# A fused attention, convolution and Fourier-mixing kernel: first batch reordered, some small operations on another engine

## The chip, the cores and the metric

The kernel runs on one core of one Trainium2 chip. The metric is the device time of one execution in microseconds (us). Before the change the median of three runs is 663.12 us (661.9 to 669.41).

The core has five engines with a queue each, worked off in order: PE (TensorE, matrix products), DVE (VectorE), ACT (ScalarE), POOL (GpSimd) and SP (SyncE, which here only issues transfers). Engines wait for each other through semaphores.

## The reference

Three parts follow each other, for four batches of 768 tokens and 384 channels (8 heads of 48):

```
f = sigmoid(f_logit)                                   # (B, H, S, D)
for t in range(S):                                     # gated linear attention
    state = f[t] * state + outer(k[t], v[t])
    y[t]  = q[t] @ state
x = y with the heads side by side                      # (B, S, 384)

gate = sigmoid(sum over 5 taps of conv_w[k] * x[t - 4 + k])
x = (gate * (x @ w_val)) @ w_out

u  = x + real(fft over tokens and channels of x)
un = (u - mean) / sqrt(var + 1e-6)
out = u + relu(un @ w_ch1) @ w_ch2                     # 384 -> 1536 -> 384
```

## The kernel before

**Attention.** Each batch is cut into six chunks of 128 tokens. The products of the decays f inside a chunk are made by `Prep` (line 405) for two chunks at a time: two ACT operations make the logarithm of f (exponential, then logarithm), a DVE scan sums it along the tokens, two more exponentials give `e` and the new `f`, and four products `scaled` multiply them into `qk` (the tile of q and k). A letter of `E0`, `E1` or `E2` (lines 1080 and 1081) says for each of the four whether DVE (v) or POOL (g) does it: `E0` for the first pair, `E1` for the second and third pair (the rest of the first batch), `E2` for all later batches. Three small operations write `ends`, `pends` and `pm`, the decay over a whole chunk. `Prep.load` fetches `f` and `qk`; there are two buffers of each, so the third pair's `qk` can be loaded only when the first pair's is read for the last time, by the outputs of the second chunk.

For a chunk, `scores` multiplies k with q and masks the result (`af` in the first batch), and `outputs` makes the change of the state, the outputs y and the new state `T`, and copies y to `xT`; a transfer moves a part of it to other partitions, and `parts` splits it into two half-precision parts `xhl`. In the first batch the products take float32 operands; `whole` transposes k on PE (tile `ktf`). In later batches operands are split into two half-precision parts (`qkhl`, `vz`), and k is transposed by a transfer (`kt`). `batch` (line 668) runs the chunks in the order: scores of the next chunk, outputs of this one, `parts` of the one before, then `others` and `ahead` for chunks further on: `others` runs the steps of the next `Prep`, `ahead` the `split` of the chunk two ahead and the load of v.

**Gates.** `gates` computes the convolution and the value product. In the first batch four of the six half gates take their convolution from PE, as products with 30 diagonal 128x128 matrices (`fs` in the profile, for the buffer they lie in). `diagonals` (line 227) makes four small vectors (`cwf`, `cwh`) and then the 30 matrices on ACT. Three half gates are done within the attention of the first batch, three in `tail`, which then makes sums and differences of the halves (`even_odd`, tiles `eo` and `gd`) and `mix`es them (Fourier products) into `u`, `un` and `unT`. ACT must load another table of functions between a sigmoid and an exponential or logarithm.

**Weights.** `small_weights` decodes `w_out` (`raw`), `w_val` (`vraw`, `wv`) and the convolution's weights from 64-bit floats, and folds tables into them (`tab`, `wth`, `wtl`, `wch`, `wp`). `mlp_weights` does the same for the 24 pieces `w` of the two large matrices: a load, three DVE operations, two on ACT and one on POOL for each piece, no more than four loads ahead.

**MLP.** `mlp` is the main part of PE's work. `merge` traces it between the attention, gates and mixing of the later batches; it starts with the first `unT`.

**What sets the order.** The program is traced in Python, and a planner then sets each engine's order ahead of time: whenever an engine is free in the planner's own simulation, it takes the ready instruction of the lowest rank, and the rank is the place in the trace. So an instruction that is ready early fills a gap, wherever it was traced. `at(c, r)` gives a block the fixed rank r instead: `LATER` (880) for the weight pieces, `LATER + 200` for the second batch's `others` and `ahead` that are traced in the first batch. `behind` and `issue_after` put an instruction behind another one of the same engine, `after` behind one of any engine. The first exponential of each `Prep` is `behind` the last ACT instruction traced so far. `aside` (line 1032) traces one step of a side job after each step of the first batch, `first` from the small weights, `second` from the pieces, `third` from the diagonals. `keep_warm` issues products with no use, 128x512 each, that keep PE active: `PRE` ahead of the first batch, `WARM` after each of its first 16 steps (`UNTIL`), `W1N` ahead of the first mix. They write a PSUM buffer `c1`, of which there are two, shared with the transposes. All instructions carry the line of a helper (L80), so the tiles tell them apart.

Of the kernel before, what the change touches and what calls it, by code (L numbers as in the profile page):

```python
# [17 lines left out]
ALU = mybir.AluOpType  # L18
# [10 lines left out]
NC = SEQ // CH  # L29
SUB = CH // 2  # L30
GW = SUB + 2
NT = 3
# [194 lines left out]
def diagonals(c):  # L227

    nc, T = c.nc, c.T
    n = KT * TAPS  # L230
    c.fs = T([128, 4, KT, DM], F16, "fs")
    c.diagonal = c.fs.rearrange("p a b d -> p (a b d)")[:, 0:2 * n * 128].rearrange("p (l k t m) -> p l k t m", l=2, k=KT, t=TAPS)
    hi, w = T([128, n], F16, "cwh"), T([128, 2, n], F32, "cwf")
    nc.gpsimd.tensor_scalar(w[:, 1], c.convw.rearrange("p a b -> p (a b)"), CW_SCALE, 1.0, ALU.mult, ALU.mult)
    nc.gpsimd.tensor_copy(hi, w[:, 1])
    nc.gpsimd.tensor_copy(w[:, 0], hi)
    nc.gpsimd.tensor_tensor(w[:, 1], w[:, 1], w[:, 0], ALU.subtract)
    for i in range(n):
        for l in range(2):
            nc.scalar.activation(c.diagonal[:, l, i // TAPS, i % TAPS], c.ident, AF.Copy, scale=w[:, l, i:i + 1])  # L240
        if i % 2:
            yield
    yield
# [68 lines left out]
def token_tables(c):  # L312

    for i in range(4):
        c.nc.gpsimd.dma_start(c.fs[:, i], c.io["fs"][i])
# [89 lines left out]
class Prep:  # L405
# [13 lines left out]
    def steps(self, es):  # L419
# [19 lines left out]
        if t == 0:  # L439
# [8 lines left out]
        cs = slice(t * TC, (t + 1) * TC)  # L448
        nc.gpsimd.tensor_copy(c.ends[:, b, :, cs, :], e[:, :, :, :, SUB + 1].rearrange("p a c h -> p h c a"))
        lo, hi = max(t * TC - 1, 0), (t + 1) * TC - 1  # L450
        pe = c.T([128, hi - lo, NP], F32, "pends", 2)
        nc.gpsimd.tensor_tensor(pe, c.ends[:, b, 1, lo:hi], c.ends[:, b, 0, lo + 1:hi + 1], ALU.mult)
        n = (hi - lo) * NP
        nc.gpsimd.tensor_tensor(
            c.pm[:, b, lo:hi].rearrange("p c a h -> p (c a) h"),
# [17 lines left out]
class Attention:  # L473


    def __init__(self, c):
        self.c = c
        self.preps, self.hl, self.kt, self.v, self.a = {}, {}, {}, {}, {}

# [172 lines left out]
    def parts(self, g, x):  # L652
# [5 lines left out]
        (nc.vector if g == NC - 1 else nc.gpsimd).tensor_tensor(x.hl[:, 1, :, s], xf, x.hl[:, 0, :, s], ALU.subtract)  # L658

    def ahead(self, g):  # L660

        if g >= NB * NC:
            return
        self.split(g)
        if g + 2 < NB * NC:
            self.load_v(g + 2)

    def batch(self, b, x, extra, others):
# [4 lines left out]
        for i in range(NC):  # L673
# [8 lines left out]
            if g + 2 < NB * NC:  # L682
                with at(c, LATER + 200 if b == 0 and g // 2 + 2 >= NT else None):
                    others(g)
                with at(c, LATER + 200 if b == 0 and g + 2 >= NC else None):
                    self.ahead(g + 2)
                if g % 2 and g // 2 + 3 < NB * NT:
                    self.prep(g // 2 + 3)
# [302 lines left out]
def emit(tc, io):  # L991
    c = setup(tc, io)
    with tc.tile_pool(name="sb", bufs=1) as pool, tc.tile_pool(name="ps", bufs=1, space=bass.MemoryType.PSUM) as psum:
# [5 lines left out]
        nc.vector.memset(c.sep.rearrange("p (a w) -> p a w", w=GW)[:, :, 0:1], 0.0)  # L999
        att = Attention(c)  # L1000
        mlp_tiles(c)
        att.prep(0)
# [12 lines left out]
        att.prep(2)  # L1015
        keep_warm(c, PRE)

# [30 lines left out]
        def abc():  # L1048
            for b in range(NB):
# [4 lines left out]
                for n, v in enumerate(att.batch(b, x, todo, others)):  # L1054
                    if b == 0:
                        aside(first, SIDE[n] if n < len(SIDE) else 1)
                        aside(third, 1, None, False)
                        if n >= WFROM:
# [8 lines left out]

                for v in tail(c, b, todo, gate, outs, hook, lambda: token_tables(c) if b == 0 else None):
                    yield v
# [10 lines left out]
E0 = 'vvvv'  # L1080
E1, E2 = 'vgvg', 'gggv'
LO = 'vgv'
# [13 lines left out]
MULTIPLIED = ((0, 0), (0, 1), (0, 2), (1, 0))  # L1096
WARM = 2
LAG = 4000.0
RATIO = 1.1
PRE = 30  # L1100
UNTIL = 16
# [353 lines left out]
```

## Time and profile before

| | |
|---|---|
| median of three runs | 663.12 us |
| the profiled execution | 660.67 us, of which 658.9 us are the span from its first to its last instruction |
| PE busy | 578.2 us (88%) |
| DVE, ACT, POOL busy | 429.9, 292.0, 218.7 us |
| mean granted PE clock | 0.950 of full speed |
| transfers | 53.40 MB, mean 81 GB/s |

The times of rows below are taken in the profiled execution, from the start of its span. "Idle before" is the time that an engine stood still ahead of a group, with what ended it; "issue" means that the profile shows nothing that it waited for. The granted clock is PE's, as a share of full speed; 0.5 is its lower level. Where nothing ran on PE yet, a clock of 1.00 has no record behind it.

### The profile page before, as it was taken

The numbers are of one execution on the slowest core, as the hardware profiler recorded it, in microseconds if no ns is written. First come the engines' busy times: TensorE is split into PE (matmuls) and PEld (weight loads), VectorE is DVE, ScalarE is ACT, GpSimd is POOL, SyncE is SP. The second block draws the span as 40 slices with busy tenths as digits, with TensorE's granted clock in tenths as the row PEclk, the third lists the DMA queues.
The fourth block names the chain that finished last, engine by engine and source line by source line (L and its number), as shares of the span: only waits on it lengthen the run. The fifth ranks groups of instructions, "written<-read, shape, count | busy, mean of one in ns | idle before, by whom it ended". The sixth has DMA issues, their size and how long they took to land.

```text
span 658.9 us, 11989 instructions
## 1 busy us (share of the span) xinstructions
PE 578.2 (88%) x4808; PEld 421.0 (64%) x4808; DVE 429.9 (65%) x710; ACT 292.0 (44%) x526; POOL 218.7 (33%) x242
## 2 busy tenths in 40 slices
PE   1477778188899889999998989999999999999995
PEld 1245666066667666777577766776577868777774
DVE  6358758796968869544669779345588493463661
ACT  3686559443477365312366663211365442121110
POOL 2175446541464361302339351212352212120000
PEclk9689789599899899999979999999999999999998
DMA  8317543922145542003205531003213100041000
GB/s 316 114 30 254 156 155 109 293 79 76 36 89 141 111 139 82 25 1 70 44 19 155 155 89 62 2 1 72 41 43 53 23 25 1 1 73 25 25 26 29
DMA packets 58098, 53.40 MB, mean 81 GB/s; under 512 B 40080, under 2 KB 49552, under 8 KB 58032
## 3 DMA queue, kind: packets, MB, share of 16 engines
q1 hardware_dynamic: 57488, 50.69, 28.0%
q0 software_dynamic: 544, 1.84, 0.9%
q8 instruction: 39, 0.64, 0.4%
q14 instruction: 27, 0.22, 0.1%
HBM read 37.58 MB, written 4.72 MB: 64 GB/s over the span
## 4 chain that ended last, share of the span: by engine, by line
PE 53%; DVE 19%; DMA 9%; issue 6%; POOL 5%; ACT 5%; SPq 1%; DVEq 0%; POOLq 0%; ACTq 0%
PE c L80 33%; PE p L80 20%; DMA qk<-in_qk 6%; DVE gate L80 5%; DVE w L80 4%; DMA w<-in_w_ch 2%; DVE eo L80 1%; DMA xT<-xT 1%; POOL w L80 1%; ACT fs L80 1%; SPq L80 1%; DVE T L80 1%; ACT f L80 1%; POOL qk L80 1%; DVE qkhl L80 1%
## 5 line engine op out<-in xcount | busy, mean ns | idle before, releaser
L80 PE MATMUL c<-unT,w 128*128 128x256 f16 x1296 | 195.6, 276 | 1.2 <-DVE unT L80 1.2
L80 PE MATMUL c<-w,hh 128*128 128x384 f16 x576 | 151.0, 328 | 2.1 <-ACT hh L80 1.3
L80 PEld LDWEIGHTS <-w 128*128 128x128 f16 x1296 | 127.0, 99 | 25.1 <-issue 1.4
L80 PE MATMUL c<-w,hl 128*128 128x384 f16 x288 | 93.0, 328 | 0.0
L80 DVE SCALAR_TENSOR_TENSOR hl<-c,hh 128x512 f16<-128x512 f32 x72 | 49.3, 685 | 62.3 <-ACT hh L80 62.1
L80 ACT ACTIVATE hh<-c 128x512 f16<-128x512 f32 x72 | 42.5, 591 | 98.5 <-PE c L80 94.7
L80 PEld LDWEIGHTS <-hh 128*128 128x128 f16 x576 | 56.2, 98 | 32.0 <-ACT hh L80 1.6
L80 PEld LDWEIGHTS <-gd 128*128 128x128 f16 x468 | 43.8, 97 | 21.7 <-issue 3.5
L80 PE MATMUL p<-wp,gd 128*128 128x388 f16 x216 | 52.7, 327 | 2.5 <-DVE xc L80 1.3
L80 PE MATMUL p<-qkhl 64*128 64x128 f16 x432 | 45.0, 227 | 6.8 <-DVE qkhl L80 5.5
L80 PE MATMUL p<-xhl,wv 128*128 128x384 f16 x216 | 44.1, 328 | 1.8 <-ACT xhl L80 1.0
L80 PE MATMUL p<-ah,vz 128*128 128x128 f16 x288 | 45.3, 228 | 0.0
L80 DVE SCALAR_TENSOR_TENSOR gate<-xT,convw,gate 128x768 f32<-128x768 f32 (+1 forms) x44 | 42.1, 1007 | 4.8 <-ACT gate L80 3.2
L80 POOL TENSOR_TENSOR xhl<-xT,xhl 128x384 f16<-128x384 f32 x23 | 25.1, 1090 | 60.3 <-ACT xhl L80 60.3
L80 PE MATMUL p<-wch,gd 128*128 128x194 f16 x252 | 41.1, 247 | 2.8 <-ACT gd L80 1.4
L80 PEld LDWEIGHTS <-wv 128*128 128x128 f16 x216 | 21.2, 98 | 32.1 <-issue 19.0
L80 PEld LDWEIGHTS <-hl 128*128 128x128 f16 x288 | 28.0, 98 | 19.9 <-issue 2.5
L80 PEld LDWEIGHTS <-qkhl 64*128 64x128 f16 x432 | 22.4, 96 | 27.9 <-issue 15.2
L80 ACT ACTIVATE f<-f 128x1056 f32<-128x1056 f32 x36 | 38.8, 1077 | 2.9 <-DMA f<-in_f 2.6
L80 POOL TENSOR_TENSOR rs<-rs,mhalf 128x2 f32<-128x2 f32 x12 | 8.4, 698 | 93.7 <-DVE rs L80 93.7
L80 PEld LDWEIGHTS <-vz 128*128 128x128 f16 x432 | 37.3, 102 | 3.3 <-issue 0.2
L80 DVE TENSOR_TENSOR a<-p,mask 128x512 f32<-128x512 f32 x36 | 23.2, 682 | 23.3 <-PE p L80 14.4
(161 smaller groups left out, 1086.9 us busy)
## 6 DMA issues: line engine op xcount, KB each, us to landing
qk<-in_qk SPq DMA_DIRECT2D x24, 512.0 KB, 5.8
w<-in_w_ch SPq DMA_DIRECT2D x21, 384.0 KB, 4.4
f<-in_f SPq DMA_DIRECT2D x12, 528.0 KB, 4.6
v<-in_v SPq DMA_DIRECT2D x24, 192.0 KB, 2.6
out_dram<-ot SPq DMA_DIRECT2D x24, 192.0 KB, 2.0
raw<-in_w_out SPq DMA_DIRECT2D x3, 384.0 KB, 4.7
vraw<-in_w_val SPq DMA_DIRECT2D x3, 384.0 KB, 7.9
xT<-xT SPq DMA_DIRECT2D x72, 16.0 KB, 1.8
```

What stands on the lines that cost most here:

```text
L80: r = f(*args, **kw)
```

## The change

The warming products are traced at the very start, ahead of the loads, and there are 20 instead of 30 (`PRE`); after each step of the first batch there is one instead of two (`WARM`). The diagonals' steps start at the sixth step of the first batch (n > 4) instead of the first. The four small operations of `diagonals` go from POOL to DVE, and so do `ends`, `pends` and `pm` of the first `Prep`, and with `E1` the four POOL products of the second and third `Prep` (two each). The first batch's `others` and `ahead` no longer have a rank of their own, but lie where they are traced, with one exception: those of the fifth and sixth chunk (NC - 2 and NC - 1, that is, the second batch's second `Prep`, and the `split` of its first two chunks) are put into a list and traced by `catch_up` only after the last gate of the first batch, with the rank 1080 that they had.

```diff
--- before.py
+++ after.py
@@ -231,10 +231,10 @@
     c.fs = T([128, 4, KT, DM], F16, "fs")
     c.diagonal = c.fs.rearrange("p a b d -> p (a b d)")[:, 0:2 * n * 128].rearrange("p (l k t m) -> p l k t m", l=2, k=KT, t=TAPS)
     hi, w = T([128, n], F16, "cwh"), T([128, 2, n], F32, "cwf")
-    nc.gpsimd.tensor_scalar(w[:, 1], c.convw.rearrange("p a b -> p (a b)"), CW_SCALE, 1.0, ALU.mult, ALU.mult)
-    nc.gpsimd.tensor_copy(hi, w[:, 1])
-    nc.gpsimd.tensor_copy(w[:, 0], hi)
-    nc.gpsimd.tensor_tensor(w[:, 1], w[:, 1], w[:, 0], ALU.subtract)
+    nc.vector.tensor_scalar(w[:, 1], c.convw.rearrange("p a b -> p (a b)"), CW_SCALE, 1.0, ALU.mult, ALU.mult)
+    nc.vector.tensor_copy(hi, w[:, 1])
+    nc.vector.tensor_copy(w[:, 0], hi)
+    nc.vector.tensor_tensor(w[:, 1], w[:, 1], w[:, 0], ALU.subtract)
     for i in range(n):
         for l in range(2):
             nc.scalar.activation(c.diagonal[:, l, i // TAPS, i % TAPS], c.ident, AF.Copy, scale=w[:, l, i:i + 1])
@@ -446,12 +446,13 @@
         scaled(0, 0, 1, e)
         scaled(1, 1, 0, e)
         cs = slice(t * TC, (t + 1) * TC)
-        nc.gpsimd.tensor_copy(c.ends[:, b, :, cs, :], e[:, :, :, :, SUB + 1].rearrange("p a c h -> p h c a"))
+        small = nc.gpsimd if self.u else nc.vector
+        small.tensor_copy(c.ends[:, b, :, cs, :], e[:, :, :, :, SUB + 1].rearrange("p a c h -> p h c a"))
         lo, hi = max(t * TC - 1, 0), (t + 1) * TC - 1
         pe = c.T([128, hi - lo, NP], F32, "pends", 2)
-        nc.gpsimd.tensor_tensor(pe, c.ends[:, b, 1, lo:hi], c.ends[:, b, 0, lo + 1:hi + 1], ALU.mult)
+        small.tensor_tensor(pe, c.ends[:, b, 1, lo:hi], c.ends[:, b, 0, lo + 1:hi + 1], ALU.mult)
         n = (hi - lo) * NP
-        nc.gpsimd.tensor_tensor(
+        small.tensor_tensor(
             c.pm[:, b, lo:hi].rearrange("p c a h -> p (c a) h"),
             pe.rearrange("p c a -> p (c a)").unsqueeze(2).to_broadcast([128, n, 2]),
             c.bmask.unsqueeze(1).to_broadcast([128, n, 2]), ALU.mult)
@@ -475,7 +476,7 @@
 
     def __init__(self, c):
         self.c = c
-        self.preps, self.hl, self.kt, self.v, self.a = {}, {}, {}, {}, {}
+        self.preps, self.hl, self.kt, self.v, self.a, self.later = {}, {}, {}, {}, {}, []
 
     def prep(self, u):
 
@@ -657,6 +658,11 @@
         nc.scalar.activation(x.hl[:, 0, :, s], xf, AF.Copy)
         (nc.vector if g == NC - 1 else nc.gpsimd).tensor_tensor(x.hl[:, 1, :, s], xf, x.hl[:, 0, :, s], ALU.subtract)
 
+    def catch_up(self):
+        for f, g in self.later:
+            f(g)
+        self.later.clear()
+
     def ahead(self, g):
 
         if g >= NB * NC:
@@ -680,10 +686,10 @@
             if i:
                 self.parts(g - 1, x)
             if g + 2 < NB * NC:
-                with at(c, LATER + 200 if b == 0 and g // 2 + 2 >= NT else None):
-                    others(g)
-                with at(c, LATER + 200 if b == 0 and g + 2 >= NC else None):
-                    self.ahead(g + 2)
+                self.later.append((others, g))
+                self.later.append((self.ahead, g + 2))
+                if g not in (NC - 2, NC - 1):
+                    self.catch_up()
                 if g % 2 and g // 2 + 3 < NB * NT:
                     self.prep(g // 2 + 3)
             yield 0
@@ -998,6 +1004,7 @@
         nc.vector.memset(c.sep, 1.0)
         nc.vector.memset(c.sep.rearrange("p (a w) -> p a w", w=GW)[:, :, 0:1], 0.0)
         att = Attention(c)
+        keep_warm(c, PRE)
         mlp_tiles(c)
         att.prep(0)
         load_constants(c)
@@ -1013,7 +1020,6 @@
         att.ahead(1)
         drain(steps[1])
         att.prep(2)
-        keep_warm(c, PRE)
 
         def others(g):
 
@@ -1054,7 +1060,7 @@
                 for n, v in enumerate(att.batch(b, x, todo, others)):
                     if b == 0:
                         aside(first, SIDE[n] if n < len(SIDE) else 1)
-                        aside(third, 1, None, False)
+                        aside(third, int(n > 4), None, False)
                         if n >= WFROM:
                             aside(second, 1, LATER)
                         if n < UNTIL:
@@ -1065,7 +1071,13 @@
                     if b == 0:
                         aside(second, WS, LATER)
 
-                for v in tail(c, b, todo, gate, outs, hook, lambda: token_tables(c) if b == 0 else None):
+                def ready():
+                    if b == 0:
+                        token_tables(c)
+                        with at(c, LATER + 200):
+                            att.catch_up()
+
+                for v in tail(c, b, todo, gate, outs, hook, ready):
                     yield v
 
         c.lag = LAG
@@ -1078,7 +1090,7 @@
 PRELOAD = (0, 3, 4, 5, 8, 11)
 DEC = 'vvvvvvvvvvvv'
 E0 = 'vvvv'
-E1, E2 = 'vgvg', 'gggv'
+E1, E2 = 'vvvv', 'gggv'
 LO = 'vgv'
 HELD = ['vector', 'scalar', 'gpsimd']
 SPO = 'vvv'
@@ -1094,10 +1106,10 @@
 WFROM = 8
 LATER = 880
 MULTIPLIED = ((0, 0), (0, 1), (0, 2), (1, 0))
-WARM = 2
+WARM = 1
 LAG = 4000.0
 RATIO = 1.1
-PRE = 30
+PRE = 20
 UNTIL = 16
 
 
```

## Rows read from the trace of the kernel before

**Rows 1.** Stretches, all engines: length; busy us of PE, PEld, DVE, ACT, POOL; clock; DMA share, GB/s.

```profile
13.30:48.40 35.10, 22.29 (x111) 14.32 (x111) 16.70 (x31) 24.02 (x57) 14.79 (x26) 0.81 0.29 103
...
93.40:97.60 4.20, 0.00 (x1) 0.00 (x0) 4.10 (x6) 2.10 (x3) 4.06 (x3) 0.65 0.22 85
97.60:112.60 15.00, 14.97 (x96) 11.99 (x97) 12.64 (x18) 13.95 (x22) 10.80 (x10) 0.87 0.34 88
112.60:128.70 16.10, 0.30 (x2) 0.07 (x1) 12.21 (x17) 7.51 (x15) 9.55 (x10) 0.58 1.03 314
...
137.10:149.70 12.60, 9.63 (x82) 6.81 (x80) 10.72 (x16) 6.46 (x17) 6.30 (x6) 1.00 0.13 37
149.70:172.70 23.00, 18.66 (x176) 13.55 (x176) 17.49 (x47) 7.38 (x18) 4.67 (x9) 1.00 0.24 70
172.70:340.00 167.30, 159.39 (x1376) 114.06 (x1376) 111.48 (x176) 77.62 (x134) 61.09 (x61) 0.96 0.29 71
```

**Rows 2.** Timeline, POOL, 0 to 50 us: start, duration, operation, [idle before].

```profile
10.47 0.72 POOL L80 COPY ends<-e 128x16 f32<-128x16 f32 x1 [6.46 <-ACT e L80]
21.51 0.19 POOL L80 TENSOR_TENSOR pends<-ends 128x4 f32<-128x4 f32 x1 [10.32 <-issue]
...
41.73 3.55 POOL L80 TENSOR_TENSOR wv<-vraw,wv 128x384 f16<-128x384 f32 x3
...
45.86 1.11 POOL L80 TENSOR_TENSOR qk<-qk,e 128x512 f32<-128x512 f32 x1
```

**Rows 3.** Timeline, ACT, 9 to 50 us.

```profile
10.81 1.07 ACT L80 ACTIVATE f<-f 128x1056 f32<-128x1056 f32 x1
22.88 5.95 ACT L80 ACTIVATE fs<-ident,cwf 128x128 f16<-128x128 f32 x20 [11.00 <-POOL cwf L80]
...
33.40 1.09 ACT L80 ACTIVATE f<-f 128x1056 f32<-128x1056 f32 x1
```

**Rows 4.** Timeline, PE, 0 to 56 us.

```profile
13.35 1.97 PE L80 MATMUL c<-ident,qk 128*128 128x128 f32 x8 [13.35 <-DVE qk L80]
...
29.36 8.54 PE L80 MATMUL c<-sep 128*128 128x512 f16 x30 [9.29 <-ACT ktf L80]
...
48.40 1.71 PE L80 MATMUL p<-qk 64*128 64x128 f32 x16 [0.80 <-POOL qk L80]
```

**Rows 5.** Timeline, DVE, 0 to 50 us.

```profile
42.30 0.89 DVE L80 TENSOR_TENSOR qk<-qk,e 128x512 f32<-128x512 f32 x1 [1.24 <-ACT e L80]
43.41 1.10 DVE L80 TENSOR_TENSOR qk<-qk,f 128x512 f32<-128x512 f32 x1 [0.22 <-ACT f L80]
```

**Rows 6.** The chain that ended last, in order of time: start, us, what.

```profile
9.64 6.89 DMA qk<-in_qk
...
55.60 5.92 DMA qk<-in_qk
```

**Rows 7.** Groups of PE, 38 to 100 us: the warming products.

```profile
L80 PE MATMUL c<-sep 128*128 128x512 f16 x32 | 9.6, 397 | 5.8 <-ACT ktf L80 4.3 <-DVE wtl L80 1.4
```

**Rows 8.** Groups of ACT, 60 to 130 us: busy, mean ns, idle before.

```profile
L80 ACT ACT_TABLE_LOAD x6 | 7.7, 1283 | 0.1
```

**Rows 9.** Timeline, ACT, 60 to 132 us.

```profile
96.01 1.28 ACT L80 ACT_TABLE_LOAD   x1
97.30 1.08 ACT L80 ACTIVATE f<-f 128x1056 f32<-128x1056 f32 x1
```

**Rows 10.** Groups of DVE, 93 to 130 us.

```profile
L80 DVE SCALAR_TENSOR_TENSOR w<-w 128x384 uint32<-128x384 uint32 x16 | 13.4, 860 | 0.3
...
L80 DVE TENSOR_TENSOR_SCAN f<-sep,f 128x1056 f32<-128x1056 f16 x1 | 2.3, 2345 | 0.0
```

**Rows 11.** Groups of POOL, 93 to 130 us.

```profile
L80 POOL TENSOR_TENSOR qk<-qk,e 128x512 f32<-128x512 f32 x4 | 6.1, 1542 | 8.4 <-DMA qk<-in_qk 8.4
```

**Rows 12.** Timeline, SP, 108 to 152 us: issues of transfers.

```profile
118.16 3.11 SPq L80 DMA_TRANSPOSE kt<-qkhl  x1
121.35 1.81 SPq L80 DMA_DIRECT2D xT<-xT  x3
```

## Prediction

> **What bounds the kernel now.** I read the page first: PE is busy for 88% of the span. The stretches come next [rows 1]. From 172.7 us on PE is busy for 159.39 of 167.3 us, so nothing but PE's work counts there, and the change leaves that work alone. What comes before can give time: there PE stands still or works off products with no use, and if the first MLP product starts earlier, the end comes as much earlier.
>
> In 13.3 to 48.4 us no engine is full: PE has 22.29 busy us of 35.1, ACT 24.02, DVE 16.70 [rows 1]. The timelines show why. POOL ends `ends` at 11.19 and starts `pends` at 21.51: 10.32 us in which the profile shows nothing that it waits for [rows 2]. Behind `pends` in its queue lie the four small operations of the diagonals. ACT waits 11.0 us for them, because the planner put 20 diagonals into a gap ahead of everything else; these take 5.95 us, 0.30 each [rows 3]. Behind them stand the copy of the transposed k, for which PE waits 9.29 us, only to run 30 warming products of no use for 8.54, and the exponential of the second pair, at 33.40 [rows 3, 4]. The last link is POOL again: its `qk` product starts only at 45.86, behind its queue of weight splits (`wv` from 41.73), and the next scores, at 48.40, wait for it [rows 2, 4]. DVE's two of the same four products were done at 44.51 [rows 5].
>
> The chain of waits then shows the third pair's `qk` load, at 55.6, issued when the second chunk's outputs release the buffer, which in PE's order stand behind those scores [rows 6]. So what the scores at 48.4 gain goes into the load and into the chunks behind it.
>
> Two more gaps follow: 93.4 to 97.6 (PE without work) and 112.6 to 128.7, 16.1 us with 0.30 of PE [rows 1]. The second batch's decays run around them.
>
> **The change part by part.** Times are against the profiled execution (660.67 us, span 658.9), which is 2.45 us below the median of 663.12.
>
> *A, the start.* With the four small operations on DVE, ACT's wait of 11.0 us goes. The diagonals before the exponential are 28 (20 in the row shown, eight between it and 33.40), 8.3 us at 0.30. Nothing but rank holds them back, so the planner may put them into the same gap; I count 2 of the 8.3. The exponential can't start much before 16.5, where the second `qk` load lands, whose `f` was issued ahead of it [rows 6]; that caps these two at 33.40 - 16.5 = 16.9. Four products on DVE in place of two add 2 x 0.9 to 1.1 us and end near 46.4, so 2 us go from 48.4. Ends: 2 (the products alone) and 18.9; I take 11 + 2 + 2 = 15, near the measured wait.
> The warming products leave PE's way between 29.36 and 37.90, but the scores wait for `qk` anyhow: nothing by themselves. At the start 20 of them, at the mean of 8.54 / 30, take 5.7 us ahead of PE's first product at 13.35 [rows 4], and at twice that still end near it. `ends`, `pends`, `pm` and the four are seven operations of 0.2 us: 1.4 us on DVE, hidden beside waits for loads; 1.4 if the cover goes.
>
> *B, half of the warming in the batch.* 16 products less. The 32 from 38 to 100 us took 9.6 us [rows 7], 0.30 each: 4.8 at most, and nothing where PE waits anyway. Against it the clock can lie lower more often: 97.6 to 112.6 ran at 0.87 after the gap at 0.65 [rows 1], and 6 us more at half speed would cost 3. Ends -4.8 and +3; I take -1.5.
>
> *C, what leaves 93 to 130 us.* ACT loads six tables in 60 to 130 us, 1.283 us each [rows 8]; with the second batch's second `Prep` behind the gates, three in all remain (one ahead of its first `Prep`, one for the gates, one behind them): 3.85 us less. Its four ACT operations (4.4 us, at 1.08 [rows 9]), DVE's scan of 2.35 [rows 10] and three POOL products of 1.54 [rows 11] go too. On SP the transpose of `kt` held 3.11 us ahead of the last `xT` transfer at 121.35, without which the gates can't start [rows 12]. DVE's weight operations took 860 ns in the mean there [rows 10]. How much of this lies on the path to 128.7, no row says. Ends: 3.85 + 4.4 + 2.35 = 10.6 gained, or 2 lost (the second batch's first `Prep`, now with an earlier rank, stands for its load at the head of DVE's queue ahead of chunk work). I take 5: SP's 3.11 and 2 of the table loads.
> After a table load ACT's next operation starts at once: 96.01 + 1.28 is 97.29, and it starts at 97.30 [rows 9]. The Trainium skill (ScalarE: Activation LUTs, "What ACT_TABLE_LOAD costs") adds a drain of some 1.38 us to each load of 1.283, 2.66 together. By it the three would be worth 8.0, and the sum 4.1 lower, an estimate; the trace has no such drain.
>
> *D, where it goes.* ACT order puts the moved `Prep` behind the last gate, on rank 1080, ahead of the sums (`eo`) and the mix. Behind it on ACT wait the `gd` copies, on DVE `eo`, on POOL the `gd` splits. In 137.1 to 172.7, ACT has 13.84 busy of 35.6, POOL 10.97, DVE 28.21 [rows 1]. So the scan and one product, 3.3 us, count on DVE, and I take 3; ends 0 and 14.2 (the slower rival). The loads of the second batch's third `Prep` and of two v tiles also move back on SP; chunks two steps into the second batch read them, and the stretch to 172.7 hides them; without that cover, one load of 5.92 [rows 6].
>
> *E, the third pair's products* all on DVE: two of 0.9 us more in series, two POOL products less beside them: +0.5, ends 0 and 1.8.
>
> *F, handed back.* Ahead of the MLP the weight pieces use DVE, and it has 12.64 of 15.0 and 12.21 of 16.1 us busy [rows 1]. That is 80%: if the pieces alone decided, 0.8 of A's 15 would come back, 12; if they move along with the batch that they are traced with, nothing. I take 3, nearer to nothing, because each piece's DVE work is held behind a batch instruction.
>
> Sum: -15 - 1.5 - 5 + 3 + 0.5 + 3 = -15, 645.7 in the profiled execution, 648 as median.
>
> **The rivals.**
> - *More* (A at 18.9, C at 10.6): -15 - 3.9 - 5.6 = -24.5, 639. For it: idle engines in all gaps. Against: the planner fills gaps, and loads take real time.
> - *The drain* of the page counts as well: 644. Against it stands 97.30.
> - *Handed back* (F at 12): -6, 657. For it: DVE and the piece loads fill 97.6 to 128.7. Against: the pieces are traced with the batch and start earlier with it.
> - *It does not do what it says*: the planner runs DVE's four small operations late and the diagonals stand in the same gap, ACT waiting as before. A is 2, the sum -2, 661.
> - *Slower*: the moved `Prep` and the `split` stand ahead of `gd` in every queue. One table load 1.28, four ACT operations 4.4, the scan 2.35, four POOL products 6.2 in series make 14.2, and two `kt` transposes of 3.11 on SP 6.2: 20.4 instead of D's 3, the sum +2.4, 666. It decides as soon as it exceeds the 18 that the rest nets. For it: rank 1080 is ahead of the mix. Against: `split` reads data that was ready long before.
>
> **How the numbers follow.** Chances: forecast 0.52 (641 to 655), more 0.13, drain 0.02, handed back 0.17 (654 to 661), not done 0.07, slower 0.09. The range 635 to 662 leaves out the lower end of "more" and most of "slower". One per cent is 6.6 us, about what a measurement of this kernel tells from no change. Faster than 656.5: 0.52 + 0.13 + 0.02 + a third of 0.17 = 0.73; slower than 669.7: the upper part of the last case, 0.06; the rest, 0.21, within.
>
> **What would show it.** A: scores of the third chunk near 33 us instead of 48.4, ACT without its 11.0 us wait, no warming products after 13.35. C: three table loads up to the mix, and a gap before the last gates near 11 us. D: `gd` no more than 3 us later behind the last gate. Wrong would be: DVE waiting for what ACT waited for, a gap of 16 us ahead of the last gates as before, or first MLP products at 170 or later.

## The result: 653.2 us, 1.25% faster, and the profile after

The changed kernel takes 653.21 us in the median of 13 runs (647.98 to 658.36), the kernel before 662.01 (13 runs): ratio 0.9875, interval 0.9849 to 0.9901. The forecast was 648 with a range of 635 to 662. The sign was right and the time is inside the range, but the largest term of the sum was far off, and what came behind it made up for a part. The profiled execution is the shortest of the 13 (647.98 us, span 646.1), so its stages show more gain than the median does; a second profile of the same kernel stands under "The kernel after once more". The profiled executions of two versions below, the warming as before and the small operations on GpSimd, are the longest of theirs (660.58 and 666.88 us), and of their stages only the start is read.

From the profile's page of the kernel after: the span and the busy time of the engines.

```profile
span 646.1 us, 11934 instructions
PE 583.7 (90%) x4782; PEld 423.4 (66%) x4782; DVE 434.5 (67%) x721; ACT 287.4 (44%) x523; POOL 212.6 (33%) x231
```

I cut both traces at the same four events: the third chunk's scores, the last gates, the first product of the mix, the first long run of MLP products. Stretches of the kernel before, cut there (columns as in [rows 1]):

```profile
48.40:128.73 80.33, 53.25 (x356) 41.22 (x357) 59.40 (x87) 51.02 (x88) 43.25 (x43) 0.83 0.62 193
128.73:149.73 21.00, 18.00 (x121) 11.25 (x121) 19.12 (x32) 10.28 (x25) 9.77 (x11) 0.92 0.29 85
149.73:172.74 23.01, 18.66 (x177) 13.55 (x177) 17.50 (x47) 7.35 (x18) 4.64 (x9) 1.00 0.24 70
172.74:658.90 486.16, 466.06 (x4045) 340.67 (x4044) 309.80 (x502) 193.21 (x336) 142.04 (x141) 0.98 0.23 56
```

The same stretches of the kernel after, and ahead of them the one up to the scores:

```profile
13.30:43.93 30.63, 15.32 (x75) 12.15 (x75) 23.09 (x41) 26.26 (x60) 14.47 (x20) 0.56 0.32 119
...
43.93:112.87 68.94, 54.22 (x347) 40.67 (x347) 45.61 (x78) 36.04 (x71) 26.88 (x28) 0.87 0.58 189
112.87:138.21 25.34, 20.67 (x122) 12.95 (x121) 23.66 (x39) 16.71 (x33) 15.33 (x13) 0.83 0.45 130
138.21:157.53 19.32, 19.01 (x164) 13.74 (x164) 15.71 (x39) 7.14 (x15) 8.59 (x13) 0.91 0.38 111
157.53:646.10 488.57, 468.38 (x4057) 341.61 (x4056) 319.89 (x513) 195.17 (x343) 143.39 (x144) 0.98 0.23 56
```

The differences are the account of this execution: -4.47 up to the scores, -11.39 from there to the last gates, +4.34 from the gates to the mix, -3.69 and +2.41 in the last two, -12.80 in all (646.1 - 658.9). In the last two PE runs 13 products fewer in the one and 12 more in the other, so they are best read together: -1.28.

The early part, where the forecast saw -15. ACT after (start, duration, operation, [idle before]), to set beside [rows 3]:

```profile
17.40 4.77 ACT L80 ACTIVATE fs<-ident,cwf 128x128 f16<-128x128 f32 x16
...
24.01 1.07 ACT L80 ACTIVATE f<-f 128x1056 f32<-128x1056 f32 x1
24.98 2.14 ACT L80 ACTIVATE fs<-ident,cwf 128x128 f16<-128x128 f32 x7
...
29.26 1.08 ACT L80 ACTIVATE f<-f 128x1056 f32<-128x1056 f32 x1
...
35.76 1.17 ACT L80 ACTIVATE e<-f,small 128x1056 f32<-128x1056 f32 x1
```

The wait of 11.0 us is gone and the second pair's exponential starts at 24.01 instead of 33.40. But the diagonals (`fs`) still run from 17.40 on, 18 of them ahead of that exponential and 12 more between it and `e` at 35.76; tracing them only from the sixth step on did not move them. Then DVE and PE, beside [rows 4, 5]:

```profile
36.95 1.67 DVE L80 TENSOR_TENSOR qk<-qk,e 128x512 f32<-128x512 f32 x2 [4.05 <-ACT e L80]
38.55 3.24 DVE L80 TENSOR_TENSOR_SCAN f<-sep,f 128x1056 f32<-128x1056 f16 x1
41.71 2.16 DVE L80 TENSOR_TENSOR qk<-qk,f 128x512 f32<-128x512 f32 x2
```

```profile
40.17 2.12 PE L80 MATMUL c<-tab,wth 128*128 128x388 f16 x6 [12.16 <-ACT wth L80]
43.93 3.09 PE L80 MATMUL p<-qk 64*128 64x128 f32 x16 [1.64 <-DVE qk L80]
...
112.87 0.48 PE L80 MATMUL p<-xhl,fs 128*128 128x384 f16 x1 [6.65 <-ACT xhl L80]
```

The third pair's scan stands between the second pair's products. PE stands still for 12.16 us, after which the 16 score products take 3.09 us instead of the 1.71 of [rows 4]: the granted clock of 13.3 to 43.93 us is 0.56, against 0.81 for the start in [rows 1]. The third row is the gap ahead of the last gates: 6.65 us, where 112.6 to 128.7 of [rows 1] had almost nothing on PE.

The lower clock reaches on to the third pair's load, which is issued 55.23 us into the kernel before and 53.29 into the kernel after. From the scores to that load PE is busy throughout; before, then after:

```profile
48.40:55.23 6.83, 6.83 (x58) 6.23 (x58) 5.64 (x7) 3.20 (x5) 1.93 (x6) 1.00 0.85 296
```

```profile
43.93:53.29 9.36, 9.36 (x56) 8.40 (x56) 5.60 (x12) 1.14 (x3) 0.42 (x2) 0.68 0.63 226
```

So of the 4.5 us at the scores 1.9 are left at the load.

### The profile page after: what moved, and what is told of

The parts are those of the page before. It is cut to its first block, busy times and chain, and to the rows that moved or that the text cites. A ratio compares the mean times of both kernels' runs of the same rounds, so it can differ in the third digit from the quotient of the medians.

```text
span 646.1 us, 11934 instructions
## 1 busy us (share of the span) xinstructions
PE 583.7 (90%) x4782; PEld 423.4 (66%) x4782; DVE 434.5 (67%) x721; ACT 287.4 (44%) x523; POOL 212.6 (33%) x231
## 4 chain that ended last, share of the span: by engine, by line
PE 53%; DVE 21%; ACT 8%; DMA 8%; issue 4%; POOL 2%; SPq 2%; DVEq 0%; ACTq 0%; POOLq 0%
PE c L80 32%; PE p L80 21%; DVE gate L80 5%; DMA qk<-in_qk 3%; DVE w L80 2%; DVE f L80 2%; DVE qk L80 2%; SPq L80 2%; DVE eo L80 2%; DMA xT<-xT 2%; DMA v<-in_v 2%; ACT fs L80 1%; DVE T L80 1%; DVE vz L80 1%; ACT f L80 1%
## 5 line engine op out<-in xcount | busy, mean ns | idle before, releaser
L80 PEld LDWEIGHTS <-gd 128*128 128x128 f16 x468 | 45.3, 101 | 26.7 <-ACT gd L80 5.0
L80 PE MATMUL p<-wp,gd 128*128 128x388 f16 x216 | 54.0, 335 | 0.9 <-DVE xc L80 0.9
L80 PE MATMUL p<-wch,gd 128*128 128x194 f16 x252 | 43.4, 258 | 6.1 <-ACT gd L80 2.9
L80 PEld LDWEIGHTS <-qkhl 64*128 64x128 f16 x432 | 22.6, 96 | 27.7 <-issue 16.1
L80 POOL TENSOR_TENSOR gd<-eo,gd 128x384 f16<-128x384 f32 x21 | 23.0, 1117 | 50.6 <-ACT gd L80 50.6
L80 POOL TENSOR_TENSOR w<-w 128x384 f16<-128x384 f32 x21 | 26.8, 1284 | 37.9 <-ACT w L80 36.7
```

Source lines behind the costliest of these rows:

```text
L80: r = f(*args, **kw)
```

## The experiments

All times are medians; ratios are to the kernel before, run on the same chip. The first theory: most of what was gained is the deferral, the start gave little. Rival: the start gave it, and the deferral only moves work.

**Without the deferral.** Everything of the change but the deferral (`catch_up` behind the gates goes too, and the second batch's first `Prep` has its old rank again):

```diff
-                self.later.append((others, g))
-                self.later.append((self.ahead, g + 2))
-                if g not in (NC - 2, NC - 1):
-                    self.catch_up()
+                with at(c, LATER + 200 if b == 0 and g // 2 + 2 >= NT else None):
+                    others(g)
+                with at(c, LATER + 200 if b == 0 and g + 2 >= NC else None):
+                    self.ahead(g + 2)
```

> The changed kernel with the second batch's decays and splits of the fifth and sixth step traced where they were before, with their old ranks; all else as changed. Theory 1 (most of the gain is the deferral: between the two traces the last gates come 15.9 us earlier, and only 6.5 of that is there at the last attention product): the gap ahead of the last gates is again 14 to 16 us instead of 6.7, the mix stage gets its 3 us back, the time is 658 to 661 us. Rival (the gain is the start and the warming, and the gap would have shrunk with any earlier start): gap below 10 us, time 652 to 655.

Measured: 654.53 us, 0.9866 [0.9826, 0.9906]: not to be told from the kernel after. The gap ahead of the last gates is 13.54 us (PE, timeline), the stage behind it 20.10.

```profile
121.89 0.48 PE L80 MATMUL p<-xhl,fs 128*128 128x384 f16 x1 [13.54 <-ACT xhl L80]
```

**The deferral alone**, the opposite edit on the kernel before:

> The kernel before with the deferral alone. Theory 1 (deferral is most of the gain): gap ahead of the last gates below 9 us instead of 16.1, mix stage 3 us longer, time 655 to 657. Rival (start and warming are the gain): 660 to 663.

Measured: 658.60 us, 0.9942 [0.9906, 0.9978]. The gap is 6.03 us (PE, timeline):

```profile
121.94 0.48 PE L80 MATMUL p<-xhl,fs 128*128 128x384 f16 x1 [6.03 <-ACT xhl L80]
```

and the stage behind it 24.24 us instead of 21.00. Neither forecast of the time came. The theory fell: the deferral takes 5 to 10 us out of the gap (13.54 against 6.65, and 8.44 in the repeat; 15.83 against 6.03) and gives 3 to 5 of them back behind it; alone it brings 0.6%, and with the fast start of this change nothing that shows.

**The warming as before**: 30 products behind the transposes, two at each step.

```diff
-        keep_warm(c, PRE)
         mlp_tiles(c)
...
         att.prep(2)
+        keep_warm(c, PRE)
...
-WARM = 1
+WARM = 2
-PRE = 20
+PRE = 30
```

> The changed kernel with the warming products as before: 30 behind the first transposes, two after each step. Theory 1: the third chunk's scores wait for the decays, not for PE, so the 30 cost nothing; the second warming product of each step costs what the stretch between the third and the fourth qk load lost, 3 us: 655 to 657. Rival (PE's 12 us without work ahead of the third chunk's scores lower the clock, and the 30 products would keep it up): 651 to 653. Second rival (the 30 products delay the first outputs by 8.5 us as before): 660 or more.

Measured: 651.62 us, 0.9821 [0.9779, 0.9863], no slower than the kernel after, so theory 1 fell. The scores start at 40.32; here the planner has the third pair's scan behind the second pair's products, which made me try that alone (below).

**The small operations back on GpSimd**, the four of the diagonals (one of them shown) and those of the first pair:

```diff
-    nc.vector.tensor_copy(hi, w[:, 1])
+    nc.gpsimd.tensor_copy(hi, w[:, 1])
...
-        small = nc.gpsimd if self.u else nc.vector
+        small = nc.gpsimd
```

> The changed kernel with the diagonals' four small operations and the first decays' three on POOL again. Theory 1: POOL stands still for some 10 us again until the first loads are through, ACT waits for it some 4 to 6 us ahead of the diagonals, the third chunk's scores come 4 to 6 us later than 43.9, and 2 to 5 us of that reach the end: 655 to 658. Rival (the start is not on the path that sets the end): 652 to 654.

Measured: 659.45 us, 0.9967 [0.9931, 1.0003]: most of the gain is gone. POOL's and ACT's timelines of this kernel:

```profile
23.12 0.19 POOL L80 TENSOR_TENSOR pends<-ends 128x4 f32<-128x4 f32 x1 [11.77 <-issue]
```

```profile
24.49 5.65 ACT L80 ACTIVATE fs<-ident,cwf 128x128 f16<-128x128 f32 x19 [12.44 <-POOL cwf L80]
```

POOL's stall and ACT's wait are back as in [rows 2, 3]; the scores come at 53.57 us and the third pair's load at 63.63 instead of 53.29, later than in the kernel before, and more of the time is lost than theory 1 said. So the small operations on DVE are a part that works.

The second theory: the start could have given more, and what it lacks is the diagonals' place (ACT) and the scan's (DVE).

**The diagonals held**, so that each engine really has them behind the batch's last instruction:

```diff
-                        aside(third, int(n > 4), None, False)
+                        aside(third, int(n > 4))
```

> The kernel after with one edit: the 30 diagonals are held, so that ScalarE's order really has them behind the work of the second pair, instead of in its early gap (17.4 to 34.6 us), where they still stand in the kernel after. Theory 1 (they fill a gap in which ScalarE waits for VectorE's chain anyway, so that their place is worth nothing): third chunk's scores at 43 to 45 us as in the kernel after (43.93), third pair's load at 53 to 54, time 652 to 655. Rival 1 (they stand in front of ScalarE's work for the second pair and are what is left of the forecast's 15 us): scores at or ahead of 41, load at or ahead of 50.5, time 648 to 651. Rival 2 (they then stand in front of the exponentials of the first batch's chunks): load as before, but last gates 2 us or more behind the kernel after (112.87), time 655 to 660.

Measured: 643.33 us, 0.9716 [0.9681, 0.9751], 9.1 us under the kernel after measured beside it (652.41); rival 1 came true, and more. This version beats both kernels. ACT, DVE and PE of this kernel:

```profile
26.58 1.18 ACT L80 ACTIVATE e<-f,small 128x1056 f32<-128x1056 f32 x1 [0.20 <-DVE f L80]
...
29.04 0.98 ACT L80 ACTIVATE fs<-ident,cwf 128x128 f16<-128x128 f32 x3
```

```profile
32.17 2.35 DVE L80 TENSOR_TENSOR_SCAN f<-sep,f 128x1056 f32<-128x1056 f16 x1
34.44 1.95 DVE L80 TENSOR_TENSOR qk<-qk,f 128x512 f32<-128x512 f32 x2
```

```profile
36.75 3.09 PE L80 MATMUL p<-qk 64*128 64x128 f32 x16
...
105.19 0.48 PE L80 MATMUL p<-xhl,fs 128*128 128x384 f16 x1 [7.70 <-ACT xhl L80]
```

`e` is 9.2 us earlier than after (35.76), the scores 7.2, the last gates 7.7: the lead stays. The third pair's scan falls into another place too: it ends at 34.52, 0.7 us behind what the product waits for from ACT (33.83), so the 9.1 us are not the diagonals' place alone.

**The diagonals from the first step on, as before**, not held; that part of the change undone alone:

```diff
-                        aside(third, int(n > 4), None, False)
+                        aside(third, 1, None, False)
```

> The kernel after with the diagonals of the convolution traced from the first step of the first batch on, as before, and not held: this one part of the change undone alone. Theory 1 (where they are traced doesn't place them; the planner puts them into ScalarE's early gap either way): the diagonals at the same places within 1 us (16 of them from 17.4 us on, 7 near 25), third chunk's scores at 43 to 44.5 us, third pair's load at 52.5 to 54.5, time within 2 us of the two runs of the kernel after (652.4 and 653.2 in the median). Rival (the later trace did some of the work, since it moves what is planned behind the diagonals): load at 56 or later, time 655 to 658.

Measured: 652.01 us, 0.9853 [0.9816, 0.9889], the scores at 43.41, the load at 52.81; ACT has the 16 diagonals at 16.88:

```profile
16.88 4.77 ACT L80 ACTIVATE fs<-ident,cwf 128x128 f16<-128x128 f32 x16
```

So that line of the change does nothing: here the planner fills the gap whenever the work is traced.

**The third pair's scan behind the second pair's products.**

```diff
-        nc.vector.tensor_tensor_scan(flat, c.sep, flat, 0.0, ALU.mult, ALU.add)
+        with c.tc.issue_after(c.scaled.ins) if self.u == 2 else ExitStack():
+            nc.vector.tensor_tensor_scan(flat, c.sep, flat, 0.0, ALU.mult, ALU.add)
...
         scaled(3, 1, 1, f)
+        c.scaled = nc.vector.last
```

> The kernel after with one edit: the scan of the third pair on VectorE is issued behind the second pair's last product, where the kernel after has it in between (38.55 to 41.8 us, ahead of the product from 41.71 on that the scores wait for). Theory 1 (VectorE's chain is what the scores wait for, and the scan is its late part): scores at 40 to 41.5 us instead of 43.93, TensorE's idle time in front of them under 10 us instead of 12.16, third pair's load at 50 to 51.5 instead of 53.29, and 2 to 3 us of it in the time, 650 to 652. Rival 1 (the third pair itself is wanted next, so what the scan gives the scores it takes from the third pair): scores earlier, load of the third pair where it was (53 to 54), time 652 to 655. Rival 2 (the scores wait for the chip's transfers or for ScalarE and not for the scan): scores at 43 or later, time 652 to 655.

Measured: 648.64 us, 0.9787 [0.9758, 0.9816], 3.8 us under the kernel after measured beside it. DVE:

```profile
39.78 2.00 DVE L80 TENSOR_TENSOR qk<-qk,f 128x512 f32<-128x512 f32 x2 [1.15 <-ACT f L80]
41.71 2.35 DVE L80 TENSOR_TENSOR_SCAN f<-sep,f 128x1056 f32<-128x1056 f16 x1
```

The scores come at 42.23, only 1.7 us earlier, since the product now waits for ACT, and the third pair's load at 52.42, 0.9 earlier. The time gained more than theory 1's 2 to 3, but the traces do not put it in the start: the last gates come at 115.48, between the two profiles of the kernel after (112.87 and 116.48). The profiled execution (647.58) is 5.0 us shorter than the repeat's; 2.2 of it are there when the MLP starts (157.89 against 160.12), and behind that 3.6 us less are lost to a lower clock (7.9 against 11.5). How much of the 3.8 belongs to the scan isn't shown.

**The second and third pair's products split as before** (`E1 = 'vgvg'` in place of `'vvvv'`). The expectation speaks of the third pair alone, but the letters of `E1` are those of both pairs:

> The kernel after with one edit: the third pair's four products go back to being split between VectorE and GpSimd (vgvg), as before. Theory 1 (the term E of the sum, +0.5 us with ends 0 and 1.8): the time is 652 to 655, third pair's load within 1 us of the kernel after (53.29). Rival 1 (on VectorE the products stand in the way of what the first chunks need, and on GpSimd they cost nothing): load at or ahead of 52, time 649 to 652. Rival 2 (GpSimd is the slower engine for them and the third pair comes late): load at 54.5 or later, time 655 to 657.

Measured: 656.26 us, 0.9893 [0.9856, 0.9931], 3.9 us more than the kernel after measured beside it (the intervals, 0.9808 to 0.9857 for that one, just touch); the load at 57.59. Rival 2's number came, with another mechanism. DVE and POOL of this kernel; the four products are the second pair's:

```profile
36.87 6.68 DVE L80 TENSOR_TENSOR_SCAN f<-sep,f 128x1056 f32<-128x1056 f16 x1
43.47 0.66 DVE L80 TENSOR_TENSOR qk<-qk,f 128x512 f32<-128x512 f32 x1
```

```profile
37.12 1.10 POOL L80 TENSOR_TENSOR qk<-qk,e 128x512 f32<-128x512 f32 x1
...
38.33 1.78 POOL L80 TENSOR_TENSOR wv<-vraw,wv 128x384 f16<-128x384 f32 x2
40.07 1.26 POOL L80 TENSOR_TENSOR qk<-qk,f 128x512 f32<-128x512 f32 x1
41.30 2.24 POOL L80 TENSOR_TENSOR pends<-ends 128x8 f32<-128x8 f32 x1
```

POOL is done with its half at 41.33. But the third pair's scan, issued at 36.87 while POOL was at work, takes 6.68 us instead of 2.35, and DVE's second product waits behind it. The scores come at 46.16, 2.2 us later, and the load 4.3 later. All of this is ahead of the third pair's own products, so the run says what the second pair's products cost on POOL, and nothing of the third pair's by themselves. The last section has what holds up the scan.

**The kernel after once more.**

> The kernel after once more, nothing changed. From the first long stretch of the MLP's products to the end the runs so far do the same work with some 20 us of idle time on TensorE, but their records show 9.9 to 25.8 us lost to a lower granted clock in stretches in which TensorE is fully busy. Theory 1 (this loss is what scatters the time between 648 and 658 us, and is not a property of a kernel): this run's start agrees with the first one's (third pair's load at 53.3 us, last gates at 112.9, first long stretch of the MLP at 157.5, each within 0.5 us), and its time differs from 647.98 by what its clock loss differs from 9.9 us, within 1.5 us. Rival (the scatter comes from transfers): the start or TensorE's idle time in the MLP differs by as much as the time does, with the clock loss equal within 2 us.

Measured: 652.41 us, 0.9832 [0.9808, 0.9857]; its profiled run 652.57. Theory 1 held in part. Of the 4.6 us between the two profiled runs, 2.6 came ahead of the MLP: the load agrees to 0.6 us (53.87), but the fourth pair's load is at 85.64 against 82.05, with a granted clock of 0.67 in 63.6 to 73.6 us where the first run had 0.80. Some 2 came behind it, 1.6 of them in lost clock (11.5 us against 9.9). The last gates are 3.6 us later, behind a longer gap:

```profile
116.48 0.48 PE L80 MATMUL p<-xhl,fs 128*128 128x384 f16 x1 [8.44 <-ACT xhl L80]
```

So a stage of a single profile is good to 3 or 4 us here. This run lies near the median of the 13, and its account against the kernel before is -4.71 up to the scores (43.69), -7.54 to the last gates, +3.72 to the mix (141.20) and +0.43 behind it: -8.10 in all, near the 8.8 of the medians.

**Combinations.** Held diagonals and the scan's edit together:

> The kernel after with the diagonals held (as in e5_diag_held) and the third pair's scan behind the second pair's last product (as in e6_scan). With the diagonals held alone that scan already stands behind the product (59.69 us against 34.44 to 36.4). Theory 1 (both edits take away the same wait, so they don't add): third chunk's scores at 36 to 38 us, third pair's load at 46 to 47.5, time 642 to 645 as with the diagonals held alone (643.33). Rival (the scan's edit also helps elsewhere, in the order that the planner then finds): load at or ahead of 45, time 639 to 642.

Measured: 649.15 us, 0.9816 [0.9760, 0.9873]; load 48.34, last gates 111.25. Both expectations missed, since I had read the wrong scan: 59.69 us is the fourth pair's. The third pair's was at 32.17, mostly in time in which DVE waited for ACT anyway; behind the product it starts at 36.72 and the third pair's `e` at 41.86 instead of 37.18. The load is 1.8 us later than with the diagonals held alone and the last gates 6.1; from the third pair's load to the fourth's it takes 31.66 us instead of 28.78, much as between the two profiles of the kernel after (31.77 and 28.76), so it isn't shown that all of the 6.1 is the scan's. A cure for one plan was no cure for the next.

Held diagonals and the warming as before:

> The kernel after with the diagonals held and the warming as before (30 products behind the second pair's transposes, two at each step instead of one). Theory 1 (the term B of the sum: warming at the front and halved is worth little either way; what it gave in e4_warm_back was the scan's place, which the held diagonals give already): time within 2 us of the diagonals held alone, 641 to 646, load at 46 to 48. Rival 1 (the third chunk's scores run at the higher clock again, 1.7 instead of 3.1 us, and TensorE is kept at it through the batch): load at or ahead of 45.5, time 639 to 641. Rival 2 (the doubled products stand in TensorE's way in the first batch): last gates 2 us or more behind the diagonals held alone (105.2), time 646 to 650.

Measured: 644.78 us, 0.9769 [0.9697, 0.9840], not to be told from the diagonals held alone. Both rivals' signs are there and cancel. The scores start at 35.58 with products of 0.1 us, and from them to the load PE is again at full clock:

```profile
35.58:41.84 6.26, 6.26 (x53) 5.78 (x52) 3.62 (x7) 6.16 (x19) 0.00 (x0) 1.00 0.68 226
```

The load is at 41.84 instead of 46.58; but from that load to the fourth pair's it takes 34.90 us instead of 28.78, and the last gates are 2.1 us later (107.32). PE's warming products in these two stretches (busy, mean ns, idle before), with the doubled warming and then with one at each step:

```profile
L80 PE MATMUL c<-sep 128*128 128x512 f16 x28 | 9.0, 417 | 4.5 <-ACT ktf L80 4.1 <-DVE wtl L80 0.3
```

```profile
L80 PE MATMUL c<-sep 128*128 128x512 f16 x14 | 5.6, 413 | 5.0 <-DVE wtl L80 4.2 <-ACT ktf L80 0.7
```

The extra 14 cost 3.4 us of PE, and the granted clock there is 0.85 with them and 0.88 without.

Held diagonals without the deferral:

> The kernel after with the diagonals held and without the deferral: the second batch's decays are traced where they were before. It tells what the deferral is worth where the start is as fast as it can be had so far. Theory 1 (the deferral takes table loads and 6 to 7 us out of the gap ahead of the last gates and gives back some 4 us in the mix behind them): without it the gap is 13 to 15 us instead of 7.70, the mix stage 20 to 21 us instead of 25.4, and the time 644 to 648 against 643.33. Rival 1 (it gives back all that it takes, and the start is all of the gain): time 641 to 644. Rival 2 (behind an early start the gap without it is longer still, since the first batch's later work is bound by ScalarE): gap over 16 us, time 648 to 653.

Measured: 648.97 us, 0.9839 [0.9785, 0.9893]; the gap is 13.15 us, the stage behind it 20.10 and the MLP starts at 152.75 instead of 149.22. Theory 1's mechanism, 1 us above its time. On the better start the deferral is worth some 1.2% (0.9716 against 0.9839, on two chips); with the change's own start it was worth nothing that shows.

## Why the prediction came out as it did, step by step

- *A, the start: -15, measured -4.5 at the scores and -1.9 at the third pair's load* (-4.7 and -1.4 in the repeat). The step that failed. ACT's wait of 11.0 us went, as said, and the exponential moved by 9.4. What failed is, first, "I count 2 of the 8.3" for the diagonals with all of the 11 on top. The planner did put them into the gap, as the prediction allowed, but there they stand ahead of the second pair's logarithm and `e` (18 before the exponential, 12 behind it): out of the way, with the scan's new place that came with it, they are worth 7.2 us at the scores and 9.1 us of the time. Second, the third pair's scan on DVE between the products, 3.24 us, was not thought of at all; moved by itself it gives 1.7 us at the scores. From the exponential to the scores it is 19.9 us (24.01 to 43.93), before 15.0 (33.40 to 48.40). Third, "nothing by themselves" for the warming products that no longer run ahead of the scores: from the scores to the load PE needs 9.36 us at a clock of 0.68 instead of 6.83 at 1.00. How much of this is the warming isn't settled: put back with the diagonals held it takes the stretch from 9.83 to 6.26, put back alone it leaves 9.96, and without it, but with the diagonals held and no deferral, it is 7.14. No experiment brought the scores to 33 either; the best was 35.58.
- *B, half of the warming: -1.5 taken.* With the diagonals held the two warmings can't be told apart (643.33 and 644.78), so near nothing; both ends of the term are seen at work, the products' cost between the loads (34.90 against 28.78) and the lower clock from the scores to the load (with the diagonals held 9.83 us under the change's warming, 6.26 under the old one).
- *C, the work ahead of the gates: -5 taken, 5 to 10 in the gap.* The gap went from 15.83 us (in the stretch of 16.1 in [rows 1]) to 6.65, 8.44 in the repeat. Without the deferral it is 13.54, so the deferral has 5.1 to 6.9 of that; with the diagonals held it has 5.5 (13.15 and 7.70), and alone, on the kernel before, 9.8 (6.03). ACT loads three tables in 60 to 130 us instead of six [rows 8], as said. The term was taken somewhat small; what took the rest of the gap isn't shown.
- *D, behind the gates: +3 taken, +4.34 measured* (25.34 against 21.00; +3.72 in the repeat, +3.2 with the deferral alone). As named, one table load, an exponential and a logarithm on ACT come between the `gd` copies, and on DVE the scan ahead of the last split:

```profile
125.57 1.28 ACT L80 ACT_TABLE_LOAD   x1
126.86 1.08 ACT L80 ACTIVATE f<-f 128x1056 f32<-128x1056 f32 x1
```

```profile
132.53 3.07 DVE L80 TENSOR_TENSOR_SCAN f<-sep,f 128x1056 f32<-128x1056 f16 x1
135.52 1.19 DVE L80 TENSOR_TENSOR gd<-eo,gd 128x384 f16<-128x384 f32 x1
```

  The last split of the kernel before:

```profile
145.88 0.54 DVE L80 TENSOR_TENSOR gd<-eo,gd 128x384 f16<-128x384 f32 x1
```

  From the last gates to the end of the last split it takes 23.8 us (112.87 to 136.71), before 17.7 (128.73 to 146.42). The prediction's own mark, `gd` no more than 3 us later behind the last gate, was missed by 3.1; the mix starts 4.34 later behind them. The slower rival's 20.4 instead of 3 did not come.
- *E, the third pair's products on DVE: +0.5 taken, not measured by itself.* The one run that undoes it undoes the second pair's too, which the prediction has in A with 2 us. That run loses 2.2 us at the scores and 4.3 at the load, before the third pair's products run, and 3.9 in the time. I counted DVE's added time and not what POOL's products do to DVE's scan.
- *F, handed back: +3 taken.* No run undoes it. Scores to last gates shrank by 11.39 us (7.54 in the repeat), so no 3 us are seen to come back as a whole; what does come back from the scores to the load (2.5) goes with the lower clock and not with the weight pieces.
- *The sum.* -15 for A, -3 for B, C, E and F, and +3 for D stand against -4.5, -11.4 and +4.3, with -1.3 behind the mix, in the first profiled run: -12.8. In the repeat they stand against -4.7, -7.5 and +3.7, with +0.4: -8.1. A's excess of 10 is made up in part by the stretch from the scores to the last gates, which shrank by 4 to 8 more than its terms. That the time lies in the range does not confirm the steps: the range is wide enough to hold A's miss even without that (648 + 10 is 658). Undone one by one, the small operations on DVE are worth some 6 us of the time (0.9967 against 0.9875) and the products on DVE 3.9; the deferral, the warming and the later diagonals are worth nothing that shows.
- *The rivals.* "It does not do what it says" came half true (the diagonals in the same gap, though ACT no longer waits for POOL). "The drain" is again not in the trace: 125.57 + 1.28 is 126.85, and the next operation starts at 126.86. The Trainium skill's sentence on it (ScalarE: Activation LUTs, "What ACT_TABLE_LOAD costs") does not hold for these loads.
- *What stays open.* Why POOL stands still for 10 to 12 us when the small operations are on it; and what besides the deferral shortened the stretch from the scores to the last gates. The two starts of the MLP lie 15.2 us apart in the first two profiles where the median gained 8.8; the repeat's lies 12.6 ahead (160.12) with more of PE's products behind it, and its end 8.1.

## What to carry to other kernels

When a planner places work by rank, tracing it later can move nothing, as here: look in the trace for where it landed, and hold it behind what it must not precede. When a long wait goes, price the queue behind it anew, for the work that the wait was hiding comes onto the path, and so does the next engine's order (here a scan between two products). Price work that is moved out of a gap on both sides: here it took 5 to 10 us out ahead of the gates, gave 3 to 5 back behind them, and was worth between nothing that shows and 1.2%. And take a second profile of the same kernel before explaining a stage: two of this one differ by 3.6 us at the last gates.

## What the runs showed of the chip

- *The scan and GpSimd.* The same scan on DVE takes between 2.35 and 6.68 us beside GpSimd work, and what goes with that is who was first. All 20 scans that took over 2.5 us by themselves in the timelines of the profiled runs began while GpSimd was at work. In the kernel after, the scan of 38.55 (3.24 us) begins behind a copy and a split of GpSimd that end at 39.57, some 2.2 us ahead of its own end. GpSimd's next operation then waits in its turn: `pends` takes 2.24 us, 0.2 elsewhere, and ends with the scan.

```profile
38.67 0.90 POOL L80 TENSOR_TENSOR wv<-vraw,wv 128x384 f16<-128x384 f32 x1
39.54 2.24 POOL L80 TENSOR_TENSOR pends<-ends 128x8 f32<-128x8 f32 x1
```

  Where the scan comes first it keeps its 2.35 us and GpSimd's operation is drawn out. With the diagonals held it runs from 32.17, and `wp`, 0.92 us elsewhere, takes 2.29:

```profile
32.94 2.29 POOL L80 TENSOR_TENSOR wp<-wpm,wp 128x388 f16<-128x388 f32 x1 [2.09 <-ACT wp L80]
```

  With `E1` as before, GpSimd's operations follow each other up to 41.33, and the scan ends 2.2 us behind that: 4.3 us of its 6.68 went by beside them. The Trainium skill (SBUF — State Buffer, "Who interferes with whom") says that a VectorE instruction with two inputs in SBUF contends with a GpSimd instruction that reads SBUF; the scan has two (`sep` and `f`), and the durations agree.
- *The clock of a busy TensorE.* Late in the kernel PE is busy throughout, yet stretches of 20 us show a granted clock below 1.00, that is, a share of them at 1.2 GHz; which ones differs between runs. The products are slower there: of those on `unT` and `w` (128x256), single ones take 0.40 us between 456 and 461 us of the second run below and 0.27 at 471.7. In the kernel after and in the held diagonals with the scan's edit:

```profile
317.50:337.50 20.00, 20.00 (x177) 14.40 (x175) 12.88 (x17) 12.76 (x21) 7.81 (x5) 0.83 0.24 53
```

```profile
456.22:476.22 20.00, 20.00 (x139) 11.78 (x138) 4.68 (x8) 7.17 (x11) 3.38 (x4) 0.67 0.18 36
```

  Adding up (1 - clock) x length from the start of the MLP to the end gives 9.9 us for the kernel after, 11.0 before, 21.2 for the second of these and between 7.9 and 25.8 over all profiled runs, at 18.7 to 22.1 us of idle time. That second run took 655.81 us, where its kernel's median is 649.15. What sets it off isn't shown; it is a reason not to judge a start by the end of a single run.
